# Attention and a two-layer MLP on one core: a join ahead of a difference on VectorE, and one burst of scores behind the first product

## The chip, the cores and the metric

The kernel runs on one core of a Trainium2 chip. The metric is the device time of one execution in microseconds (us). A core has a matrix engine (PE, with its weight loads shown apart as PEld), VectorE (DVE), ScalarE (ACT), GpSimd (POOL) and a queue engine (SP) that here only issues DMAs. Each engine runs its own instructions in program order and waits for the others through semaphores.

## The reference

Eight batches of 12 heads of attention, 448 tokens, head size 64, and then a two-layer MLP with a leaky ReLU over the 3584 rows that come out:

```python
scores = scale * np.matmul(q, k.transpose(0, 1, 3, 2))      # scale = 1/8
attn = softmax(scores)                                       # over the last axis
x = np.matmul(attn, v)      # heads side by side: 3584 x 768
h = x @ w_in                # 768 x 2048
g = np.maximum(0.01 * h, h)
out = g @ w_out             # 2048 x 768, float32
```

## The kernel before, in words

**Units and ranges.** Attention is done by units of two heads: 48 units, each of 4 chunks of scores (112 rows of keys, both heads). The rows of the MLP are done in 7 ranges of tokens, `cuts = [0, 640, 1152, 1664, 2176, 2688, 3072, 3584]`, numbered 0 to 6. Range 0 has 640 tokens, range 5 has 384, the others 512. A range is a short one in this text's code where it has fewer than 512 tokens (`short`, in `block_pair`); the planner's new condition also counts the last range in. While one range is in its second layer, the attention of the ranges after it is computed between its matmuls, so that the exponentials on ACT have matmuls of the MLP beside them.

**First layer.** `hidden(i)` computes h for range i from x transposed (`xT`), by a scheme with seven products in place of eight: blocks of x, and of the weights, are added to and subtracted from each other ahead of the products (`mix_x_part` on DVE, L416, writes `x_mix`). `mix_h` (L441, L442) forms the sums of h that the second layer needs.

**Second layer.** `block_pair(i, c)` computes two blocks of 128 tokens at once, o1 and o2 of 768 columns each, and again with seven products in place of eight. A product is 8 matmuls of 128x384 (L541), with h as the weights that are loaded and `w_out_sb` or its mixed form `w_mix` streaming. There are two PSUM banks for the results, a and b. In the code's order the products write b, a, b, a, b, a, b; products 3, 5, 6 and 7 add onto what their bank holds already. In between, DVE takes the banks' values into o: `keep` copies (L546), `join` adds (L549). `h[:, lo, one]` is overwritten by a difference after product 1 (L553), and `h[:, hi, one]`, which product 2 reads and product 6 reads again, by a difference after product 2 (L558). In the first pair of a short range or of the last range, the `keep` behind product 1 runs on ACT, in all others on DVE. Range 0 has one pair of this kind behind a pair without the scheme (`plain_pair`), the other six ranges have two each: 13 pairs.

A bank may be written again only when what it held has been read: product 3 waits for the `keep` behind product 1, product 4 for the join behind product 2, product 7 for the join behind product 5. DVE runs its queue in order, so an instruction waits for everything queued ahead of it, L416's wait for a transposed x among it.

**Attention between the products.** `second(i)` walks through the pairs of a range. `block_pair` yields after every quarter of a product (two matmuls), and at each yield `place` may put in work for attention: a *burst* of three chunks of scores (six matmuls on PE, L271, into three score tiles of PSUM, and three exponentials on ACT, L280), or the *rows* of one unit (32 matmuls of attention times v, L789, then a reciprocal and a multiply on DVE, L795 and L796, and DMA transposes of x issued on SP, L237). A burst also needs its unit's q and k transposed, by a DMA transpose issued on SP. POOL casts q, k and v and issues the loads.

When a burst is placed is decided when the program is built, by a small model of time in the planner: `model["now"]` grows by 0.325 at each quarter of a product and by 0.78 at a burst, and `free` says for each score tile when it is thought to be free again. `plan = [9, 8, 8, 8, 8, 5, 0]` is the number of bursts that each range is to hold. At the start of each range from 1 on, the model is set back to 0 and every tile's `free` to one value, which is what the second edit changes. A burst is placed when

```python
want > done and state < 2 and turned(last) and not blocked and len(slots) == 3 and all(
    x <= now + 0.05 + 0.2 * j for j, x in enumerate(at)
)
```

with `at` the three tiles' `free` values.

Of the kernel before, what the change touches and what calls it, by code (L numbers as in the profile page):

```python
# [16 lines left out]
def kernel(  # L17
# [13 lines left out]
    P = 128  # L31
# [9 lines left out]
    cuts = [0, 640, 1152, 1664, 2176, 2688, 3072, B * S]  # L41
    NR = len(cuts) - 1
# [24 lines left out]
    slots = [ps_s.tile([P, 2, 512], F32, name=f"sc{i}") for i in range(3)]  # L67
# [253 lines left out]
    def store(o, t0, cols=slice(0, DM), queues=(nc.sync, nc.sync)):  # L321

        queues = list(queues)
        done = 0
        while done < P:
            b, j = divmod(t0 + done, S)
            so, p = divmod(j, SC)
            n = min(SC - p, P - done)
            dst = out[b * S:(b + 1) * S].rearrange("(p so) n -> so p n", so=NSC)
            queues.pop(0).dma_start(out=dst[so, p:p + n, cols], in_=o[done:done + n, cols])  # L330
            done += n
# [87 lines left out]
    def spots(i):  # L419

        if i == 0:
            return 0, [(0, 1), (2, 3)]
        return 0, [(0, 2), (1, 3)] if cuts[i + 1] - cuts[i] == 4 * P else [(0, 1), (KEEP, 2)]

    def token(i, x):

        return KEEP * P if x == KEEP else cuts[i] + x * P
# [96 lines left out]
    def block_pair(i, c):  # L524

        lo, hi = slice(0, MH), slice(MH, MD)
        x1, x2 = spots(i)[1][c]
        one, two = ts(x1, P), ts(x2, P)
        s3 = h_mix[:, :, c]
        t2, t3, t4 = (w_mix[:, x] for x in range(3))  # L530
        t1 = w_out_sb[:, lo, NW:]
        left, right = slice(0, NW), slice(NW, DM)
        o1 = o_pool.tile([P, DM], F32, name="o")
        o2 = o_pool.tile([P, DM], F32, name="o")
        b, a = banks

        def product(ps, x, w, first=False, cols=slice(0, NW)):
            for m in range(MH):
                if m in (2, 4, 6):
                    yield  # L540
                nc.tensor.matmul(  # L541
                    ps[:, cols], x[:, m], w[:, m], start=(first and m == 0), stop=(m == MH - 1), skip_group_check=True,
                )

        def keep(o, at, ps, by=nc.vector.tensor_copy):
            by(o[:, at], ps[:, :NW])  # L546

        def join(o, at, ps):
            nc.vector.tensor_add(o[:, at], o[:, at], ps[:, :NW])  # L549

        yield
        yield from product(b, h[:, lo, one], w_out_sb[:, lo, left], first=True)
        nc.vector.tensor_sub(h[:, lo, one], h[:, lo, two], h[:, lo, one])  # L553
        short = cuts[i + 1] - cuts[i] < 4 * P
        keep(o1, left, b, nc.scalar.copy if c == 0 and (short or i + 1 == NR) else nc.vector.tensor_copy)
        yield
        yield from product(a, h[:, hi, one], w_out_sb[:, hi, left], first=True)
        nc.vector.tensor_sub(h[:, hi, one], h[:, hi, one], h[:, lo, one])  # L558
        join(o1, left, a)
        yield  # L560
        yield from product(b, h[:, lo, one], t2)
        keep(o1, right, b)
        yield
        yield from product(a, h[:, lo, two], t1, first=True)
        keep(o2, right, a)
        yield
        yield from product(b, s3, t3)
        join(o2, right, b)
        yield
        t0 = token(i, x2)  # L570
        last = t0 + P == B * S
        if last:
            nc.vector.tensor_copy(o2[:, NW // 2:NW], b[:, NW // 2:NW])
            store(o1, token(i, x1), left)
            store(o2, t0, right)
        yield from product(a, h[:, hi, one], w_out_sb[:, hi, right])
        join(o1, right, a)
        store(o1, token(i, x1), right if last else slice(0, DM))
        yield
        if last:  # L580
            w1, w2 = slice(0, NW // 2), slice(NW // 2, NW)
            yield from product(b, h[:, hi, two], t4[:, :, w1], cols=w1)
            nc.vector.tensor_copy(o2[:, w1], b[:, w1])
            store(o2, t0, w1, (nc.scalar, nc.sync))
            end = slots[0][:, 0]
            yield from product(end, h[:, hi, two], t4[:, :, w2], first=True, cols=w2)
            nc.vector.tensor_add(o2[:, w2], o2[:, w2], end[:, w2])
            store(o2, t0, w2, (nc.scalar, nc.sync))
            return
        yield from product(b, h[:, hi, two], t4)  # L590
        keep(o2, left, b)
        store(o2, t0)
        banks.reverse()
# [138 lines left out]
    a, b = idle[:, 0], idle[:, 1]  # L732
# [25 lines left out]
    def advance():  # L758
        nonlocal tick
        tick += 1  # L760
        u = to["turn"]
        if u < min(NU, chunk // NSC + NQ, to["cast"]):
            dma_transposes(u)
            to["turn"] += 1
        u = to["cast"]
        if u < min(NU, to["turn"] + 2, to["load"][0], to["load"][1]):
            cast(u, (0, 1))
            to["cast"] += 1
        u = to["v"]
        if u < min(NU, rows_done + NV, to["load"][2]):  # L770
            cast(u, (2,))
            to["v"] += 1
        if tick % 2 == 0:
            x = min(range(3), key=lambda x: to["load"][x])
            u = to["load"][x]
            if u < NU and u - 3 < (to["cast"], to["cast"], to["v"])[x]:
                load_soft(u, 2, (x,))
                to["load"][x] += 2

    def rows():  # L780
        nonlocal rows_done
        u = rows_done
        e, vt = e_sb[u % NE], v_sb[u % NV]
        ps = next_slot()[:, :, :NSC * (D + 1)].rearrange("p j (q d) -> p j q d", q=NSC)
        for j in range(2):
            for qc in range(NSC):
                for c in range(NSC):
                    at = (j * NSC + c) * S + qc * SC
                    nc.tensor.matmul(  # L789
                        ps[:, j, qc, :], e[:, at:at + P], vt[:, j, c, :],  # L790
                        start=(c == 0), stop=(c == NSC - 1),
                    )
        x_t[u] = x_pool.tile([SC, NSC, 2, D], BF16, name="x")
        rec = r_pool.tile([SC, 2, NSC, 1], F32, name="rec2")
        nc.vector.reciprocal(rec, ps[:SC, :, :, D:])  # L795
        nc.vector.tensor_mul(  # L796
            x_t[u].rearrange("p q j d -> p j q d"), ps[:SC, :, :, :D], rec.to_broadcast([SC, 2, NSC, D])
        )
        if u in X_PE:
            owed_x.append((u, model["now"] + 2.0))  # L800
        else:
            x_transposes(u)
        rows_done += 1
# [66 lines left out]
    model = {"now": 0.0, "act": 0.0, "free": {}, "ready": {}}  # L870
# [57 lines left out]
    def second(i):  # L928
# [4 lines left out]
        for c in range(len(spots(i)[1])):  # L933
            whole = c < plain(i)
            for x, _ in enumerate((plain_pair if whole else block_pair)(i, c)):
                fine = 1 if whole else 2
                if x % (2 * fine) == 0:
                    advance()
                if c or x:
                    model["now"] += 0.65 / fine  # L940
                left -= place(i, left, calm=whole or x not in (1, 2), keen=need[min(i + 2, NR)], cap=NU if all(summed) else need[i + 2])
                if whole and x in (1, 3, 5, 7):
                    mix_h(i, x - 1)
                if whole and x in (8, 9, 11, 13, 15):
                    next(outs)
                if i == 0 and c and x % 4 == 2:
                    next(ins, None)
                for y in range(2):
                    if fresh[y] is None and i + 1 < NR and rows_done >= need[i + 2] - 1 + y:
                        fresh[y] = model["now"] + 7.0  # L950
                for y, todo in enumerate(x_sums if x % fine == 0 else ()):
                    if fresh[y] is not None and fresh[y] <= model["now"] and not summed[y]:
                        summed[y] = next(todo, 0) is not None
                        if not summed[y]:
                            break
# [30 lines left out]
    for i in range(1, NR):  # L986
        for step, _ in enumerate(hidden(i)):
            advance()
            if step % 4 == 2 and NSC * (rows_done + 1) <= chunk:
                rows()  # L990
        model.update(now=0.0, act=2.3, free={id(x): 0.9 for x in slots}, ready={})
        second(i)


# [28 lines left out]
```

## Time and profile before

| | |
|---|---|
| time, median of 3 runs | 390.14 us (388.68 to 390.62) |
| time of the profiled execution | 388.9 us |
| span from its first to its last instruction | 387.1 us |
| mean granted clock of TensorE | 0.998 |
| exponentials (L280, ACT) | 192, 163.1 us, mean 918 ns |
| difference L558 (DVE, 128x1024 bf16) | 13, 681 to 1124 ns, median 691 |
| join L549 (DVE, 128x384) | 39, 540 to 555 ns, median 553 |
| keep L546 on DVE / on ACT | 49, median 557 ns / 2, 479 and 492 ns |
| transpose of x or of q and k (SP queue) | one issue takes about 1.2 us |
| loads of q, k, v | 224 KB each, 5.6 to 6.6 us from issue to landing (median) |

The span is counted from the first instruction to the last; the time has what lies around it as well. A line of the timeline gives the start and the duration in us, the engine, the line of the kernel, what is written and read, the number of instructions that are merged in it, and in brackets the idle time of the engine ahead of it with what ended it. TensorE's matmuls overlap, so a merged line's duration is a little longer than the time after which the next one starts; the distance of two starts is the measure. A wait for several semaphores is put down to the one that came last.

### The profile page before, as it was taken

What the parts mean: (1) busy time and instruction counts of PE and PEld (TensorE: products, weight loads), DVE (VectorE), ACT (ScalarE), POOL (GpSimd) and SP (SyncE); (2) the same over time, 40 slices, a digit from 0 to 9 for tenths busy, and PEclk for the clock granted to TensorE, in tenths of its full rate; (3) what the DMA queues carried; (4) which work ended last, traced back from release to release, by engine and by line L of the source; (5) the groups of instructions that cost most, each with busy time, mean ns of one, the idle gap of its engine ahead of it and who ended that gap; (6) DMA issues with size and microseconds to landing.
All of it is one profiled execution on the core that took longest, in us unless ns stands there. A gap on an engine that the chain in (4) does not pass through costs nothing.

```text
span 387.1 us, 10006 instructions
## 1 busy us (share of the span) xinstructions
PE 378.1 (98%) x4093; PEld 262.1 (68%) x4093; DVE 232.7 (60%) x489; ACT 264.9 (68%) x391; POOL 139.9 (36%) x222
## 2 busy tenths in 40 slices
PE   8899999999999999999999999999999999999996
PEld 3565657766588555886558865688656894668854
DVE  3653848566766645766468664665745674464754
ACT  5998885765768776588765887668777686708700
POOL 8797640865537233620436204363042100000000
PEclk9999999999999999999999999999999999999999
DMA  8999999999997969981599815999158500421023
GB/s 131 194 200 203 178 201 182 109 126 199 167 170 91 120 119 137 216 100 25 119 154 180 119 25 93 172 166 141 25 58 192 120 14 1 107 58 50 3 76 88
DMA packets 93246, 46.75 MB, mean 121 GB/s; under 512 B 51856, under 2 KB 89872, under 8 KB 93200
## 3 DMA queue, kind: packets, MB, share of 16 engines
q0 software_dynamic: 38224, 22.58, 46.1%
q1 hardware_dynamic: 54912, 23.50, 31.1%
q8 instruction: 32, 0.52, 0.6%
q14 instruction: 14, 0.11, 0.1%
q10 hardware_dynamic: 64, 0.02, 0.0%
HBM read 45.61 MB, written 11.01 MB: 146 GB/s over the span
## 4 chain that ended last, share of the span: by engine, by line
PE 92%; DVE 2%; DMA 2%; ACT 1%; POOL 1%; issue 1%; POOLq 0%; DVEq 0%; ACTq 0%
PE g L541 31%; PE g L469 14%; PE sc L469 14%; PE sc L789 11%; PE sc L271 10%; PE g L352 4%; PE g L606 3%; PE g L647 2%; DMA w_in_mix<-in_k_dram 2%; PE g L290 2%; PE g L254 1%; ACT e L280 1%; POOL w_in_mix L141 1%; PE sc L352 1%; DVE x L298 1%
## 5 line engine op out<-in xcount | busy, mean ns | idle before, releaser
L280 ACT ACTIVATE e<-sc 112x896 bf16<-112x896 f32 x192 | 163.1, 918 | 50.9 <-PE sc L271 50.7
L541 PEld LDWEIGHTS <-h 128*128 128x128 bf16 x632 | 57.3, 98 | 46.4 <-issue 14.8
L541 PE MATMUL g<-w_out_sb,h 128*128 128x384 bf16 x416 | 80.9, 326 | 0.6 <-DVE o L549 0.6
L458 ACT ACTIVATE h<-c 128x512 bf16<-128x512 f32 (+1 forms) x72 | 43.5, 611 | 25.9 <-DVE c L484 17.3
L469 PEld LDWEIGHTS <-w_in_sb 128*128 128x128 bf16 x576 | 54.3, 98 | 6.0
L789 PEld LDWEIGHTS <-e 112*128 112x128 bf16 x1344 | 48.2, 98 | 4.9 <-ACT e L280 0.7
L172 POOL COPY v<-fv 112x512 bf16<-112x512 bf16 x38 | 24.5, 657 | 74.6 <-PE sc L789 74.6
L271 PE MATMUL sc<-qkT 64*128 64x448 bf16 x384 | 49.9, 355 | 0.7 <-DVE qkT L260 0.5
L789 PE MATMUL sc<-v,e 112*128 112x65 bf16 x1344 | 49.8, 194 | 0.4 <-ACT e L280 0.4
L170 POOL COPY qkb<-fq 112x512 bf16<-112x512 bf16 x38 | 25.1, 660 | 69.0 <-DMA fq<-in_q_dram 38.4
L469 PEld LDWEIGHTS <-w_in_mix 128*128 128x128 bf16 x432 | 41.2, 98 | 4.1
L546 DVE COPY o<-g 128x384 f32<-128x384 f32 x49 | 27.2, 554 | 23.4 <-PE g L541 23.3
L541 PE MATMUL g<-w_mix,h 128*128 128x384 bf16 (+1 forms) x208 | 38.3, 323 | 0.9 <-ACT o L546 0.9
L795 DVE RECIPROCAL rec<-sc 112x8 f32<-112x8 f32 x42 | 8.7, 207 | 42.5 <-PE sc L789 26.9
L271 PEld LDWEIGHTS <-qkT 64*128 64x128 bf16 x384 | 15.4, 94 | 26.6 <-issue 18.7
L170 POOL COPY qkb<-fk 112x512 bf16<-112x512 bf16 x38 | 24.4, 641 | 16.3 <-DMA fk<-in_k_dram 16.3
L549 DVE TENSOR_TENSOR o<-o,g 128x384 f32<-128x384 f32 x39 | 21.5, 551 | 14.2 <-PE g L541 14.1
L796 DVE TENSOR_TENSOR x<-sc,rec 112x512 bf16<-112x512 f32 x42 | 29.0, 691 | 1.7 <-DVE rec L795 0.3
L469 PE MATMUL g<-xT,w_in_sb 128*128 128x256 bf16 (+1 forms) x216 | 28.5, 268 | 0.0
L469 PE MATMUL sc<-xT,w_in_sb 128*128 128x256 bf16 (+1 forms) x216 | 28.5, 268 | 0.0
L541 PE MATMUL g<-w_mix,hmix 128*128 128x384 bf16 x104 | 20.1, 326 | 0.0
L469 PE MATMUL g<-x_mix,w_in_mix 128*128 128x256 bf16 (+1 forms) x144 | 19.0, 268 | 0.0
(102 smaller groups left out, 476.6 us busy)
## 6 DMA issues: line engine op xcount, KB each, us to landing
fq<-in_q_dram POOLq DMA_DIRECT2D x19, 224.0 KB, 5.7
fk<-in_k_dram POOLq DMA_DIRECT2D x19, 224.0 KB, 6.6
fv<-in_v_dram POOLq DMA_DIRECT2D x19, 224.0 KB, 5.6
w_in_sb<-in_moe_w_in_dram POOLq DMA_DIRECT2D x4, 768.0 KB, 11.9
w_out_sb<-in_moe_w_out_dram POOLq DMA_DIRECT2D x4, 768.0 KB, 18.6
out_dram<-o SPq DMA_DIRECT2D x7, 336.0 KB, 4.2
out_dram<-o SPq DMA_DIRECT2D x8, 288.0 KB, 3.3
out_dram<-o SPq DMA_DIRECT2D x7, 240.0 KB, 3.4
```

The costliest lines, as they stand in the source:

```text
L170: by(qk_sb[u][:, x].rearrange("p so h d -> p h so d"), f)
L172: by(v_sb[u % NV][:, :, :, :D], f)
L271: nc.tensor.matmul(ps[:, j, :S], t[j * D:(j + 1) * D, S + c * SC:S + c * SC + P], t[j * D:(j + 1) * D, :S], start=True, stop=True,)
L280: nc.scalar.activation(e[:, :, c, :], sc_t.pop((u, c))[:SC, :, :S], AX.Exp, scale=scale)
L352: nc.tensor.matmul(open_t[m][:, :n], w_in_sb[:, kk, ts(m, P)], xT[:, kk, at:at + n], start=(fresh and kk == kks[0]), stop=(kk == KD - 1),)
L458: nc.scalar.activation(hs[:, m:m + 2, cols], x.rearrange("p (m t) -> p m t", m=2), AX.Prelu, alpha=0.01)
L469: nc.tensor.matmul(ps[:, j * nh:(j + 1) * nh], w[:, kk, ts(j, P)], x[:, kk], start=(first and j == 0 and kk == 0), stop=(kk == KH - 1), sk ...
L541: nc.tensor.matmul(ps[:, cols], x[:, m], w[:, m], start=(first and m == 0), stop=(m == MH - 1), skip_group_check=True,)
L546: by(o[:, at], ps[:, :NW])
L549: nc.vector.tensor_add(o[:, at], o[:, at], ps[:, :NW])
L789: nc.tensor.matmul(ps[:, j, qc, :], e[:, at:at + P], vt[:, j, c, :], start=(c == 0), stop=(c == NSC - 1),)
L796: nc.vector.tensor_mul(x_t[u].rearrange("p q j d -> p j q d"), ps[:SC, :, :, :D], rec.to_broadcast([SC, 2, NSC, D]))
```

## The change

Two edits. In `block_pair`, the join behind product 2 is issued ahead of the difference that overwrites `h[:, hi, one]`; both are on DVE, and nothing is added or left out. In the loop over ranges 1 to 6, the value that the planner gives to the three score tiles at a range's second layer is 0.9 for a range of 512 tokens that isn't the last, as before, and 1.2 for the other two (range 5 with 384 tokens, and range 6, the last).

```diff
         keep(o1, left, b, nc.scalar.copy if c == 0 and (short or i + 1 == NR) else nc.vector.tensor_copy)
         yield
         yield from product(a, h[:, hi, one], w_out_sb[:, hi, left], first=True)
+        join(o1, left, a)
         nc.vector.tensor_sub(h[:, hi, one], h[:, hi, one], h[:, lo, one])
-        join(o1, left, a)
         yield
...
-        model.update(now=0.0, act=2.3, free={id(x): 0.9 for x in slots}, ready={})
+        model.update(now=0.0, act=2.3, free={id(x): 0.9 if cuts[i + 1] - cuts[i] == 4 * P and i + 1 < NR else 1.2 for x in slots}, ready={})
         second(i)
```

The order of the instructions follows from it: on DVE the two instructions change places in each of the 13 pairs. On PE one burst moves, the first one of range 5: two matmuls of product 1 (with their weight loads) that stood behind the burst's six now stand ahead of them. On ACT the copy of o's left half in that pair, which stood behind the burst's three exponentials, stands ahead of them. The orders on POOL and on SP are the same.

## The prediction

> **What bounds the kernel now.** I read the page first, then the chain that ended last, then the waits by engine, and last the timeline around each wait of TensorE that names the two places of the change.
>
> ```profile
> PE 378.1 (98%) x4093; PEld 262.1 (68%) x4093; DVE 232.7 (60%) x489; ACT 264.9 (68%) x391; POOL 139.9 (36%) x222
> PE 92%; DVE 2%; DMA 2%; ACT 1%; POOL 1%; issue 1%; POOLq 0%; DVEq 0%; ACTq 0%
> ...
> PE g L541 <- ACT o L546: 0.9, 1, 0.9
> PE g L541 <- DVE o L549: 0.6, 2, 0.4
> ```
>
> TensorE is the bound: 98% busy, 92% of the chain. DVE and ACT have a third of the span to spare, so moving their work pays only where TensorE waits for it. The last two lines (waits of TensorE: total, times, longest) are all that this view charges to the two orders the change touches: one wait for ACT's copy of o's left half (L546), two for DVE's join (L549). So it is a matter of one or two microseconds, and the timeline must give them exactly.
>
> A product is 8 matmuls. Undisturbed products in the last range start at 368.98, 370.28, 371.58 and 372.88: 1.30 us each, 0.1625 a matmul. A pair's products are numbered 1 to 7 in program order; 1, 3, 5 and 7 write bank b, the others bank a. The join of product 2 must have read a before product 4 may write it. In before it stands behind the difference L558. The four places where TensorE then loses time (start, duration, engine, line):
>
> ```profile
> 96.14 1.46 PE L541 MATMUL g<-w_mix,h 128*128 128x384 bf16 x8
> 96.34 1.12 DVE L558 TENSOR_TENSOR h<-h 128x1024 bf16<-128x1024 bf16 x1 [0.45 <-PE g L541]
> 97.39 0.54 DVE L549 TENSOR_TENSOR o<-o,g 128x384 f32<-128x384 f32 x1
> 97.98 0.48 PE L541 MATMUL g<-w_out_sb,h 128*128 128x384 bf16 x2 [0.38 <-DVE o L549]
> ...
> 320.27 2.53 ACT L280 ACTIVATE e<-sc 112x896 bf16<-112x896 f32 x3 [0.44 <-PE sc L271]
> 320.54 1.80 PE L541 MATMUL g<-w_out_sb,h 128*128 128x384 bf16 x10
> 322.68 0.49 ACT L546 COPY o<-g 128x384 f32<-128x384 f32 x1
> 323.23 1.46 PE L541 MATMUL g<-w_mix,h 128*128 128x384 bf16 x8 [0.89 <-ACT o L546]
> ...
> 339.71 1.46 PE L541 MATMUL g<-w_mix,h 128*128 128x384 bf16 x8
> 340.78 0.55 DVE L549 TENSOR_TENSOR o<-o,g 128x384 f32<-128x384 f32 x1
> 341.38 1.46 PE L541 MATMUL g<-w_out_sb,h 128*128 128x384 bf16 x8 [0.20 <-DVE o L549]
> ...
> 367.51 1.46 PE L541 MATMUL g<-w_mix,h 128*128 128x384 bf16 x8
> 368.38 0.55 DVE L549 TENSOR_TENSOR o<-o,g 128x384 f32<-128x384 f32 x1
> ```
>
> See that product 3 began at 96.14 and was due to hand over at 97.44, but product 4 began at 97.98, right after a join that ended at 97.93.
>
> **Part one, the join ahead of the difference.** It swaps two DVE instructions in each of 13 pairs; nothing is added. The join starts when the difference did and ends one difference earlier (0.69, or 1.12 at 96.34). Where TensorE waited, it stops waiting:
>
> - first range: 97.98 - (96.14 + 1.30) = 0.54. New join 96.34 to 96.89, before 97.44.
> - range 5 (384 tokens), second pair: 341.38 - (339.71 + 1.30) = 0.37. New join 340.18 to 340.73, before 341.01.
> - last range, first pair: 368.98 - (367.51 + 1.30) = 0.17. New join 367.77 to 368.32, before 368.81.
>
> In the other ten pairs the join is early enough, or a burst of scores stands between products 3 and 4, or (range 5, first pair) TensorE waits earlier: worth nothing. The difference itself ends 0.55 later. Its reader is product 6, over 2.5 us behind; the copy of o's right half queued behind it ends when it did, as the two together take as long as before. If that cover were gone, product 5 would wait at most 0.55 a pair.
>
> Now the 0.54 at 98. What is late next there is DVE's own queue. L416 waits for a transpose of x, and the join of product 5 is queued behind it:
>
> ```profile
> 103.08 0.82 DVE L416 TENSOR_TENSOR x_mix<-xT 128x512 bf16<-128x512 bf16 x1 [0.33 <-DMA xT<-x]
> 103.16 1.46 PE L541 MATMUL g<-w_out_sb,h 128*128 128x384 bf16 x8
> 103.82 0.54 DVE L549 TENSOR_TENSOR o<-o,g 128x384 f32<-128x384 f32 x1
> ```
>
> The transposes behind L416 were issued on SP by 97.55, from x that DVE finished at 95.42, ahead of the changed join, so their landing does not move. That join ends at 104.36 as before; product 7, which writes b, was to start at 103.16 + 1.30 = 104.46, and would now be ready at 103.92. It waits until about 104.41. Of 0.54, 0.05 is left. Between the ends 0.05 and 0.54 I take 0.05, since these rows are the place itself.
>
> The Trainium skill, "SBUF — State Buffer", section "SBUF: two separate sides", has a rule against the swap here: a VectorE instruction with two SBUF inputs and a GpSimd one that reads SBUF take a shared port exclusively, and the loser waits for the whole instruction. The difference has two SBUF inputs, and moved to 96.85 it would meet POOL's copy of v at 96.86 (its duration here is 1.07, elsewhere 0.62). The row agrees that they disturb each other (1.12 at 96.34 against a median of 0.691). By the rule the difference would end at 96.86 + 0.62 + 0.69 = 98.17, by the row at 97.97; the copy behind it is not needed before product 5, over 1 us later, so the sum is the same by both.
>
> **Part two, the threshold 0.9 to 1.2.** The planner's clock starts at 0 and goes on by 0.325 at each quarter of a product. At 0.9 the burst fits after three quarters (0.975), at 1.2 only after the whole (1.3). Of the two ranges named, the last has a plan of 0 bursts, so only range 5 changes: two matmuls of product 1 move ahead of the burst (six weight loads and six score matmuls), and on ACT the copy of o's left half moves ahead of the burst's three exponentials. No DMA, no POOL and no SP instruction moves.
>
> Before: copy at 322.68, behind 2.53 us of exponentials; product 3 was due at 320.54 + 10 x 0.1625 = 322.17 and started at 323.23: 1.06 lost. After: product 1 ends its issue at 320.10, its last matmul is through by about 320.30, the copy takes 320.30 to 320.79, and product 3 starts at 322.17. The whole 1.06 is won.
>
> The new price: the exponentials start about 0.42 later and end about 323.22 instead of 322.80, while the second burst comes at 323.56 instead of 324.62. Its three score tiles are released at about 321.6, 322.4 and 323.22 and wanted at 323.56, 323.76 and 323.95: at least 0.73 spare, so nothing. Bounds: 0, and 0.42 if all of that lateness reached TensorE; I take 0 by these rows. Downstream from here no load is outstanding: POOL has no instruction between 318 and 346, and SP's transposes of this stretch start behind the rows they turn. Everything moves with TensorE.
>
> One row is doubtful: the reciprocal at 327.92 starts about 0.36 after the exponential it waits for ends (327.56). Through its multiply, ended at 328.85, it holds the last score tile of the third burst until 328.91, 0.15 late. I take it to move along. If it is tied to time and not to its inputs, TensorE gives 1.06 back there.
>
> **Sum.** 0.05 + 1.06 + 0.37 + 0.17 = 1.65 us off a profiled execution of 388.9 (span 387.1 to 385.45): 387.25, or 0.42%. That execution is 1.24 below the median of the three runs; I carry the difference over to the median: 390.14 - 1.65 = 388.5.
>
> **Rivals.**
>
> - A, nothing is absorbed at 104. Against it: the 0.33 wait of L416. For it: that transpose took 5.5 us from issue to landing, where a lone one at 338.94 took 2.4, so it can land sooner. Then 0.54 counts whole, 2.14 in all, and with the 0.15 at 328.9 gone too 2.29: 387.9 to 388.0.
> - B, the time saved at 322 is given back at 328.9 as above: 1.65 - 1.06 = 0.59, so 389.5. For it: the reciprocal's unexplained 0.36. Against: the same row in the ranges before follows its exponential within 0.02.
> - C, slower: at the same L416 the transposes land later, because POOL's two loads (issued 97.89 and 98.58) get ahead of them when POOL's copies shift beside the moved difference. It decides once the landing is later by more than 1.65, past 104.7. With one load's median of 5.7 us on top of 103.05, TensorE loses 5.7 - 1.65 = 4.1 net: 394.2; at half of that, 391.3. Against: the turn of x is issued 0.34 ahead of the first load.
> - D, the second part does less than it says. That holds for the last range already and is in the sum; for range 5 the order of the instructions decides it.
>
> **How the numbers follow.** Forecast 0.58, A 0.22, B 0.12, C 0.08. Faster by over 0.5% (about what a measurement of this kernel can tell from no change) needs 1.95 us. The forecast stands 0.30 short of that, less than the 0.48 between two of the three runs before: I give it 0.22 faster and 0.36 same. A is just beyond: 0.17 and 0.05. B is 0.12 same, C 0.08 slower. Faster 0.39, same 0.53, slower 0.08. The range reaches down to A less the 1.46 by which the lowest run lies below the median, 386.4, and up to B with the bound of 0.42 and the 0.48 of the highest run, 390.4; C is left out; the forecast's own is 387.0 to 389.0.
>
> **What would show it.** In the profile after: ACT's copy of o ahead of the burst's exponentials near 320.3, no wait of TensorE for L546, and product 3 of that pair following product 2 without a gap; joins ahead of the differences, and no wait of TensorE for a join near 98, 341 or 369; a gap of about half a microsecond before product 7 near 104.4. I am wrong if the second burst near 323.5 waits for an exponential, if the third near 327.5 to 329 holds TensorE by over 0.3, or if L416 near 103 waits for much longer than 0.9.

## The result, and the profile after

The changed kernel took 387.68 us, median of 8 runs, against 389.81 for the kernel before: ratio 0.9941, 95% interval 0.9921 to 0.9961, so 0.59% faster. One of the eight, of 392.64 us, was a slow run that the ratio leaves out; the median of the other seven is 387.56. Measured twice more beside the experiments below, the changed kernel gave ratios of 0.9963 (0.9940 to 0.9987) and 0.9950 (0.9924 to 0.9976). The three agree within their intervals, around half a per cent, which is 1.9 us.

The profiled execution took 388.12, with a span of 386.4, only 0.8 less than before. Where the time went is not read from the two spans but from TensorE's own starts. From the page after, its engines and its chain; then the head of its waits of TensorE:

```profile
PE 378.3 (98%) x4093; PEld 262.8 (68%) x4093; DVE 232.0 (60%) x489; ACT 264.7 (69%) x391; POOL 141.5 (37%) x222
...
PE 94%; DMA 2%; DVE 1%; POOL 1%; ACT 1%; issue 1%; POOLq 0%; DVEq 0%; ACTq 0%
```

```profile
PE g L207 <- DVE gate L202: 1.2, 1, 1.2
PE g L254 <- DVE qkb L170: 1.0, 1, 1.0
PE sc L271 <- DVE qkT L260: 0.5, 1, 0.5
```

The two waits of L541 (for ACT's copy and for the join) are gone from the list. A wait of 1.0 at L254, long before the first changed instruction, was 0.2 before; it ended at 11.95 us, 0.33 later than in the profile before. The windows from 10 to 20 us show what followed it; their columns are the stretch, its length, busy time and count of PE, PEld, DVE, ACT and POOL, then TensorE's granted clock, the DMA share and GB/s. First before, then after:

```profile
10.00:15.00 5.00, 4.03 (x69) 2.79 (x70) 2.85 (x10) 4.84 (x7) 2.56 (x5) 1.00 1.41 187
15.00:20.00 5.00, 4.83 (x83) 3.07 (x81) 3.37 (x11) 4.59 (x7) 5.00 (x9) 1.00 1.29 204
```

```profile
10.00:15.00 5.00, 3.77 (x47) 2.21 (x44) 2.35 (x8) 3.57 (x5) 2.22 (x4) 0.74 1.44 195
15.00:20.00 5.00, 4.83 (x84) 3.48 (x81) 3.27 (x10) 4.38 (x6) 5.00 (x9) 0.92 1.30 204
```

The clock stood at 0.74 and 0.92 where it was 1.00 before; in windows of half a microsecond it was 0.50 from 12.5 to 15.5 us. By 16 us TensorE was 1.1 us late, and it stayed so. Product 1 of the first changed pair shows it, in the timeline before and then in the timeline after:

```profile
91.73 1.46 PE L541 MATMUL g<-w_out_sb,h 128*128 128x384 bf16 x8
```

```profile
92.81 1.46 PE L541 MATMUL g<-w_out_sb,h 128*128 128x384 bf16 x8
```

It starts 1.08 later. From that product to the end of the span the kernel before took 295.4 us and the changed one 293.5, which is 1.9 less. The places where the prediction saw TensorE wait, in the timeline after (start, duration, engine, line; near 98, 104, 322, 341 and 369):

```profile
97.33 1.46 PE L541 MATMUL g<-w_mix,h 128*128 128x384 bf16 x8
97.53 0.56 DVE L549 TENSOR_TENSOR o<-o,g 128x384 f32<-128x384 f32 x1 [0.42 <-PE g L541]
98.63 0.49 PE L541 MATMUL g<-w_out_sb,h 128*128 128x384 bf16 x2
...
103.32 0.42 DVE L416 TENSOR_TENSOR x_mix<-xT 128x512 bf16<-128x512 bf16 x1
103.81 1.46 PE L541 MATMUL g<-w_out_sb,h 128*128 128x384 bf16 x8
104.02 0.56 DVE L549 TENSOR_TENSOR o<-o,g 128x384 f32<-128x384 f32 x1 [0.28 <-PE g L541]
105.11 0.49 PE L541 MATMUL g<-w_mix,h 128*128 128x384 bf16 x2
```

```profile
319.48 1.46 PE L541 MATMUL g<-w_out_sb,h 128*128 128x384 bf16 x8
320.98 0.48 ACT L546 COPY o<-g 128x384 f32<-128x384 f32 x1 [0.46 <-PE g L541]
321.35 2.54 ACT L280 ACTIVATE e<-sc 112x896 bf16<-112x896 f32 x3
321.55 1.48 PE L541 MATMUL g<-w_out_sb,h 128*128 128x384 bf16 x8
322.86 1.46 PE L541 MATMUL g<-w_mix,h 128*128 128x384 bf16 x8
324.25 0.74 PE L271 MATMUL sc<-qkT 64*128 64x448 bf16 x6
```

```profile
339.37 1.46 PE L541 MATMUL g<-w_mix,h 128*128 128x384 bf16 x8
339.84 0.55 DVE L549 TENSOR_TENSOR o<-o,g 128x384 f32<-128x384 f32 x1
340.67 1.46 PE L541 MATMUL g<-w_out_sb,h 128*128 128x384 bf16 x8
...
366.81 1.46 PE L541 MATMUL g<-w_mix,h 128*128 128x384 bf16 x8
367.07 0.56 DVE L549 TENSOR_TENSOR o<-o,g 128x384 f32<-128x384 f32 x1 [0.49 <-PE g L541]
368.11 1.46 PE L541 MATMUL g<-w_out_sb,h 128*128 128x384 bf16 x8
```

See the distances of starts: 97.33 to 98.63, 103.81 to 105.11, 321.55 to 322.86, 339.37 to 340.67 and 366.81 to 368.11 are all 1.30 or 1.31. TensorE loses nothing at any of the five, and the copy of o stands ahead of the exponentials. How late a matmul is against the same matmul of before falls from 1.19 to 0.65 at product 4 near 98, from 0.67 to -0.37 at product 3 near 322, to -0.71 near 341 and to -0.87 near 369: 0.54 + 1.04 + 0.34 + 0.16 = 2.1 us. Elsewhere 0.2 was lost in this execution (0.11 of it at a burst near 96, before any changed instruction).

### The profile page after: what moved, and what is told of

It is laid out like the page before. It is cut to its first block, busy times and chain, and to the rows that moved or that the text cites. A ratio compares the mean times of both kernels' runs of the same rounds, so it can differ in the third digit from the quotient of the medians.

```text
span 386.4 us, 10006 instructions
## 1 busy us (share of the span) xinstructions
PE 378.3 (98%) x4093; PEld 262.8 (68%) x4093; DVE 232.0 (60%) x489; ACT 264.7 (69%) x391; POOL 141.5 (37%) x222
## 4 chain that ended last, share of the span: by engine, by line
PE 94%; DMA 2%; DVE 1%; POOL 1%; ACT 1%; issue 1%; POOLq 0%; DVEq 0%; ACTq 0%
PE g L541 32%; PE g L469 14%; PE sc L469 14%; PE sc L789 11%; PE sc L271 10%; PE g L352 4%; PE g L606 3%; PE g L647 2%; DMA w_in_mix<-in_k_dram 2%; PE g L290 2%; PE g L254 1%; POOL w_in_mix L141 1%; PE sc L352 1%; PE g L317 1%; DVE x L298 0%
## 5 line engine op out<-in xcount | busy, mean ns | idle before, releaser
L541 PEld LDWEIGHTS <-h 128*128 128x128 bf16 x632 | 57.3, 98 | 44.3 <-issue 12.5
L541 PE MATMUL g<-w_out_sb,h 128*128 128x384 bf16 x416 | 80.9, 326 | 0.0
L170 POOL COPY qkb<-fq 112x512 bf16<-112x512 bf16 x38 | 26.0, 684 | 68.2 <-DMA fq<-in_q_dram 37.4
L541 PE MATMUL g<-w_mix,h 128*128 128x384 bf16 (+1 forms) x208 | 38.3, 323 | 0.0
L271 PEld LDWEIGHTS <-qkT 64*128 64x128 bf16 x384 | 15.5, 94 | 26.8 <-issue 18.3
L541 PE MATMUL g<-w_mix,hmix 128*128 128x384 bf16 x104 | 20.1, 326 | 0.0
```

What stands on the lines that cost most here:

```text
L170: by(qk_sb[u][:, x].rearrange("p so h d -> p h so d"), f)
L271: nc.tensor.matmul(ps[:, j, :S], t[j * D:(j + 1) * D, S + c * SC:S + c * SC + P], t[j * D:(j + 1) * D, :S], start=True, stop=True,)
L541: nc.tensor.matmul(ps[:, cols], x[:, m], w[:, m], start=(first and m == 0), stop=(m == MH - 1), skip_group_check=True,)
```

## The experiments

The theory: TensorE's waits at the four places add up, and nothing else is gained. Rivals: the DVE order helps in all 13 pairs; the burst's place, not ACT's queue, is what counts; part of the gain is given back near 104. All runs were profiled, and what each place cost TensorE can be read in each: the distance of two products' starts less 1.30, or for product 3 its lateness behind product 2. Anything up to 0.02 is given as 0.

| kernel | 98: product 4 | 104: product 7 | 322: product 3 | 341: product 4 | 369: product 4 |
|---|---|---|---|---|---|
| before | 0.54 | 0 | 1.05 | 0.37 | 0.17 |
| after | 0 | 0 | 0 | 0 | 0 |
| join alone | 0 | 2.02 | 1.05 | 0 | 0 |
| burst alone | 0.46 | 0 | 0 | 0.37 | 0.17 |
| both, second profile | 0 | 0 | 0 | 0 | 0 |
| both, third profile | 0 | 0 | 0 | 0 | 0 |
| copy on DVE in range 5 | 0.11 | 0 | 0.11 | 0.36 | 0.17 |
| ACT's copy in ranges 1 to 4 too | 0.57 | 0 | 1.05 (five times) | 0.37 | 0.17 |
| short treatment everywhere | 0 | 0 | 0 | 0 | 0 |
| both, product 5's join ahead of L416 | 0 | 0 | 0 | 0 | 0 |
| short treatment and that join | 0 | 0 | 0 | 0 | 0 |

### The burst alone

```diff
-        model.update(now=0.0, act=2.3, free={id(x): 0.9 for x in slots}, ready={})
+        model.update(now=0.0, act=2.3, free={id(x): 0.9 if cuts[i + 1] - cuts[i] == 4 * P and i + 1 < NR else 1.2 for x in slots}, ready={})
```

> Only the second part: the first burst of range 5 behind product 1, joins behind the differences as before. Theory: 1.06 us off, all of it at product 3 near 322; the joins near 98, 341 and 369 hold TensorE by 0.54, 0.37 and 0.17 as before. Rival (the exponentials that now end 0.42 later hold the second or third burst): 0.6 or less off, with a new wait between 323 and 329.

Measured: 387.57 us against 389.07, ratio 0.9967 (0.9948 to 0.9986), so about 1.3 us. In its profile the lateness against the kernel before falls from 0.69 to -0.35 at product 3 near 322, 1.04, and nowhere else behind the first 20 us by more than 0.1; the later exponentials hold no burst. The theory holds.

### The join alone

```diff
+        join(o1, left, a)
         nc.vector.tensor_sub(h[:, hi, one], h[:, hi, one], h[:, lo, one])
-        join(o1, left, a)
```

> Only the first part: the join ahead of the difference in all 13 pairs, the burst where it was. Theory (waits of TensorE add up; the one near 98 us is as long as POOL makes the difference there: 0.54 where it took 1.12 us, 0.11 where it took 0.69): no wait for a join near 98, 341 and 369, so 0.65 to 1.08 us off, with product 3 near 322 still 1.06 late. Rival (the DVE order helps in all pairs): more than 1.6 us off, with differences spread over the ranges.

Measured: 388.52 us against 388.8, ratio 0.9995 (0.9974 to 1.0017). The waits for a join near 98, 341 and 369 are gone and the one near 322 stands at 1.05, as expected, and there is no gain in other pairs. But the profiled execution, the slowest of its twelve (391.97), lost 2.02 at product 7 of range 0. Its timeline there:

```profile
104.64 1.46 PE L541 MATMUL g<-w_out_sb,h 128*128 128x384 bf16 x8
...
106.79 0.65 DVE L416 TENSOR_TENSOR x_mix<-xT 128x512 bf16<-128x512 bf16 x1 [2.56 <-DMA xT<-x]
...
107.36 0.54 DVE L549 TENSOR_TENSOR o<-o,g 128x384 f32<-128x384 f32 x1
...
107.96 0.48 PE L541 MATMUL g<-w_mix,h 128*128 128x384 bf16 x2 [1.85 <-DVE o L549]
```

DVE stood 2.56 at L416 for a transpose of x, with the join of product 5 queued behind it, and TensorE stood 1.85 for that join. This is the prediction's chain at 104, in full, in another execution than the one it was read from. It is also the execution with the lowest early clock of all that were profiled (0.61 from 10 to 15 us, 0.71 from 15 to 20); that the one brings the other is not shown.

The ratio does not resolve the gain, but the clock helps. The mean granted clock of an execution is known for all of them, and 7 of these 12 were below 0.998, against 3 of 19 of the kernel before on this chip. Among those at 0.998 or above, the join alone has a median of 387.82 (5 executions) and the kernel before 388.70 (16): 0.9 us, inside the 0.65 to 1.08 that the places allow. This choice was made after the runs, and 5 are few. Whether an earlier join makes the late transpose more frequent is not shown: it held TensorE in one of the profiles with the join ahead and in none of the others.

### Both again, twice

> The changed kernel once more, for a second profile. Theory: the two parts add up, 2.1 us off where L416 near 103 finds its transpose landed, 1.65 us off where it waits for it and the join of product 5 holds product 7. Rival (the 2.1 of the first profile hung on that execution's late start): near 104 TensorE loses about 0.4 again in an execution whose first range does not start late.

> The changed kernel on the same chip as the kernel with the short ranges' treatment everywhere. Theory: 1.7 to 2.1 us below the kernel before, by how long POOL made the difference near 98 in the kernel before; no wait of TensorE for ACT's copy or for a join, and none of 0.4 at product 7 near 104. Rival (the last part of the gain is given back near 104): a gap there of 0.3 or more.

Measured: 387.8 us against 389.07, ratio 0.9963 (0.9940 to 0.9987), and 386.5 against 388.8, ratio 0.9950 (0.9924 to 0.9976). At a clock of 0.998 or above alone, the medians are 386.58 (4) against 388.78 (19, with one of 1326.82 us left out), 2.2 less, and 386.35 (6) against 388.70 (16), 2.3 less; for the burst alone, 387.42 (10) against the same 388.78, it is 1.4. The third profile, whose early clock is 1.00, answers the question of the late start, since at the burst ahead of product 3 it stands at the same time as the kernel before (0.05 earlier). From there the lateness goes to -0.58 at product 4, to -1.62 near 322, to -1.98 and to -2.15: 0.53 + 1.04 + 0.36 + 0.17 = 2.1, and the span ends 2.1 earlier. Its timeline near 104:

```profile
102.08 0.42 DVE L416 TENSOR_TENSOR x_mix<-xT 128x512 bf16<-128x512 bf16 x1
...
102.58 1.46 PE L541 MATMUL g<-w_out_sb,h 128*128 128x384 bf16 x8
102.78 0.56 DVE L549 TENSOR_TENSOR o<-o,g 128x384 f32<-128x384 f32 x1 [0.28 <-PE g L541]
...
103.88 0.49 PE L541 MATMUL g<-w_mix,h 128*128 128x384 bf16 x2
```

L416 did not wait at all, took 0.42 in place of 0.82, and the join ran as soon as product 5 was through. Nothing is given back. In the second profile L416 did wait (0.28, to 104.13), and product 7 still followed product 6 by 1.30.

### The copy on DVE, the burst left where it was

```diff
-        keep(o1, left, b, nc.scalar.copy if c == 0 and (short or i + 1 == NR) else nc.vector.tensor_copy)
+        keep(o1, left, b, nc.scalar.copy if c == 0 and i + 1 == NR else nc.vector.tensor_copy)
```

> The kernel before, with one copy moved: in range 5, first pair, o's left half is copied by DVE and not by ACT; the burst stays where it was. Theory (TensorE waited for a copy that stood in ACT's queue behind three exponentials): product 3 starts about 0.13 late in place of 1.06, so 0.9 us off, though no burst moves. Rival (the place of the burst among the matmuls is what counts): less than 0.3 us off.

Measured: 388.36 us against 389.07, ratio 0.9978 (0.9953 to 1.0003): the time alone does not decide. The profile does. Its timeline near 322:

```profile
320.84 2.53 ACT L280 ACTIVATE e<-sc 112x896 bf16<-112x896 f32 x3 [0.44 <-PE sc L271]
...
321.11 1.80 PE L541 MATMUL g<-w_out_sb,h 128*128 128x384 bf16 x10
...
322.25 0.55 DVE L546 COPY o<-g 128x384 f32<-128x384 f32 x1
322.85 1.46 PE L541 MATMUL g<-w_mix,h 128*128 128x384 bf16 x8
```

The burst and its exponentials are where they were, yet product 3 starts 0.11 late and not 1.05. It was ACT's queue, not the place of the scores among the matmuls.

### The same wait at four more places

```diff
-        keep(o1, left, b, nc.scalar.copy if c == 0 and (short or i + 1 == NR) else nc.vector.tensor_copy)
+        keep(o1, left, b, nc.scalar.copy if c == 0 else nc.vector.tensor_copy)
```

> The kernel before, with the suspected wait put in at four more places: in ranges 1 to 4 too the first pair's left half of o is copied by ACT, whose queue then holds the burst's three exponentials ahead of it; bursts and joins as before. Theory: product 3 of these four pairs starts 1.06 late in place of 0.11, so 3.8 us slower, 1.0%. Rival (the wait near 322 came from something of range 5 alone, such as its narrower blocks): less than 1 us slower.

Measured: 392.81 us against 388.8, ratio 1.0103 (1.0076 to 1.0130), 4.0 us slower. From its waits of TensorE (total, times, longest):

```profile
PE g L541 <- ACT o L546: 4.4, 5, 0.9
```

Before it was 0.9, once. Five places of the same price (1.05 each by the starts, 0.11 of which the four new ones had before): 4 x 0.94 = 3.8 by the profile, 4.0 by the time. So the wait is not peculiar to range 5.

### The short ranges' treatment everywhere

```diff
-        keep(o1, left, b, nc.scalar.copy if c == 0 and (short or i + 1 == NR) else nc.vector.tensor_copy)
+        keep(o1, left, b, nc.scalar.copy if c == 0 or i + 1 == NR else nc.vector.tensor_copy)
...
-        model.update(now=0.0, act=2.3, free={id(x): 0.9 if cuts[i + 1] - cuts[i] == 4 * P and i + 1 < NR else 1.2 for x in slots}, ready={})
+        model.update(now=0.0, act=2.3, free={id(x): 1.2 for x in slots}, ready={})
```

> The changed kernel with the short ranges' treatment in all of ranges 1 to 6: the first burst behind product 1 (threshold 1.2) and o's left half copied by ACT ahead of it; in the last range the second pair's copy is on ACT too. Theory: the 0.11 that product 3 still waits for DVE's copy near 131, 180, 229, 278 and 376 goes, so 0.55 us below the changed kernel, or more where the wait near 131 is longer. Rival (the exponentials of four more ranges now end 0.4 later and hold the second burst): slower than the changed kernel.

Measured: 385.9 us against 388.8, ratio 0.9934 (0.9909 to 0.9959), 0.6 us below the changed kernel of the same chip (386.5). Its timeline in range 1:

```profile
127.74 0.48 ACT L546 COPY o<-g 128x384 f32<-128x384 f32 x1 [0.35 <-PE g L541]
...
128.12 2.54 ACT L280 ACTIVATE e<-sc 112x896 bf16<-112x896 f32 x3
...
128.31 1.47 PE L541 MATMUL g<-w_out_sb,h 128*128 128x384 bf16 x8
...
129.62 1.46 PE L541 MATMUL g<-w_mix,h 128*128 128x384 bf16 x8
```

Product 3 follows product 2 by 1.31. The 0.11 that the copy on DVE, behind its difference, cost near 131, 180, 229, 278 and 376 is gone at all five, and no later burst waits. Near 131 that wait was not always 0.11: it was 0.15 in the profile after, 0.31 in the burst alone and 0.55 in the second profile of both together, so there the treatment is worth more in some executions.

### The join of product 5 ahead of L416

In the changed kernel, and in the one with the short treatment everywhere, one number of the planner is raised so that in range 0 the join of product 5 stands ahead of the first L416 on DVE; no other engine's order changes.

```diff
-                        fresh[y] = model["now"] + 7.0
+                        fresh[y] = model["now"] + (7.0 if i else 8.0)
```

> The changed kernel with one more step moved on DVE: in range 0 the join of product 5 stands ahead of the first L416, which waits for a transpose of x, and not behind it. Theory (L416's wait, where the transpose lands late, reaches TensorE through that join, 2.0 us in the execution of the join alone): no wait of TensorE at product 7 in any execution, however long L416 waits; the lowest time as for the changed kernel, near 386, and fewer runs above 388. Rival (the late transposes hold TensorE elsewhere, at product 3 of range 1's first layer or at a join behind it): as many high runs as for the changed kernel, and the wait of TensorE moves to about 106 to 109.

> The short ranges' treatment in all of ranges 1 to 6 and the join of product 5 ahead of L416 in range 0, together. Theory: the two add up, 2.6 to 3.1 us below the kernel before, ratio 0.992 to 0.9935, median at most that of the short ranges' treatment alone. Rival: no lower than the changed kernel, 0.994 to 0.996.

Measured: the first 386.79 us against 388.74, ratio 0.9943 (0.9920 to 0.9965), its six runs from 386.54 to 387.26; the second 385.68, ratio 0.9915 (0.9889 to 0.9941), from 385.13 to 386.37. The changed kernel's two later measurements reached 389.92 and 389.3, but those were executions with a clock of 0.991 and 0.990, and all twelve here stood at 0.998 or above: the narrower spread says nothing for the earlier join. In both profiles TensorE waits at none of the five places. In the second the transpose was in time. In the first it landed at 103.31, 0.68 after product 6 had started:

```profile
102.63 1.46 PE L541 MATMUL g<-w_out_sb,h 128*128 128x384 bf16 x8
102.83 0.56 DVE L549 TENSOR_TENSOR o<-o,g 128x384 f32<-128x384 f32 x1 [0.61 <-PE g L541]
103.33 0.43 DVE L416 TENSOR_TENSOR x_mix<-xT 128x512 bf16<-128x512 bf16 x1
...
103.93 0.49 PE L541 MATMUL g<-w_mix,h 128*128 128x384 bf16 x2
```

L416 began as soon as its transpose had landed, with the join already through, and product 7 followed product 6 by 1.30. With L416 ahead of the join, as in the changed kernel, the join would have started near 103.8 and ended near 104.3, and product 7 would have been 0.4 to 0.5 late: an estimate from these rows. So the earlier join was worth that much in this execution, and nothing in the one where the transpose was in time. The second kernel has the lowest ratio of all, 0.85% below the kernel before, but its interval overlaps that of the short treatment alone (0.9909 to 0.9959): the times don't show that the two gains add up.

## Why the prediction was right or wrong

Its time, 388.5 with a range of 386.4 to 390.4, held the result of 387.68. The likeliest case was 0.42% faster; measured were 0.59%, 0.37% and 0.50%. Right in kind, short by one term. Of the 0.8 us between 388.5 and 387.68, 0.33 lies in the kernel before, whose median was 390.14 in the three runs that the prediction started from and 389.81 in the eight of the result; the rest, 0.49, is about that term.

- **The wait for ACT's copy near 322, 1.06.** Right: 1.04 in the burst alone and in the third profile, and its cause is shown by moving the copy to DVE and by repeating the wait four times.
- **The joins near 341 and 369, 0.37 and 0.17.** Right: 0.34 to 0.36 and 0.16 to 0.17.
- **"Of 0.54, 0.05 is left."** This is the step that failed: all three profiles of the changed kernel keep the whole of it, 0.53 to 0.54 where it can be read against the kernel before, so the sum was 2.1 and not 1.65. The chain was right, as the execution with 2.02 shows. Its premise was not, that the landing of the transpose "does not move". In the three profiles L416 began 0.49, 0.14 and 0.50 ahead of product 6, where in before it was 0.08, and it took 0.42 to 0.49 in place of 0.82. One execution's landing and one long L416 were taken for constants. It was not the new order that moved them: in the three other profiles with the join behind the difference (the burst alone, the copy on DVE, ACT's copy in more ranges) L416 also began 0.49 to 0.50 ahead of product 6, waited for no transpose and took 0.42. The transpose took 5.5 us from issue to landing in the profile before, and from 4.7 to 7.1 over all eleven profiles; and the L416 of 0.82 ran beside a copy of POOL's (103.00 to 103.62). Rival A was the case.
- **Nothing for the later exponentials.** Right: in the profile after they end at 323.89 and the third tile is wanted near 324.64, 0.75 spare against the 0.73 foreseen.
- **Nothing for the difference behind the join.** Right: no instruction waits for it in any profile.
- **Rival B, the reciprocal tied to time.** Fell: it moved along, still 0.37 to 0.39 behind its exponential; see the last section.
- **Rival C, slower through a late transpose.** Its place was right and its effect occurs, but not as the usual case: in one of the nine profiles of the experiments, and by the estimate above it would have cost 0.4 to 0.5 in one more. Its reason, loads that get ahead, does not decide it alone: in that execution one load was issued ahead of the transpose (99.27 against 99.63) and the transpose took 7.1 us, but in the second profile of both together it was issued first (97.08 against 97.51) and took 7.0. Why it lands when it does is left open.
- **The Trainium skill, "SBUF — State Buffer", section "SBUF: two separate sides".** Its rule is that a VectorE instruction with two SBUF inputs and GpSimd's copy exclude each other and the one that starts first holds the port. By that rule and the prediction's own starts (96.85 for the difference, 96.86 for the copy) the difference would have held it; the 98.17 was worked out as if POOL did. The traces agree in so far as the two hold each other up: the moved difference took 1.75 us beside three of POOL's copies, of which two kept their 0.62 and the third took 1.08 (the short treatment everywhere), and 0.69 in the third profile of both together, where the copy that began behind it took 1.08. Which of the two holds the port was not to be read from the starts, as in both the difference is shown to begin 0.03 to 0.08 ahead of the copy. As foreseen, nothing on the path waited for it.

On the chances: forecast and rival A lie 0.5 us apart, on either side of the bound of 0.5%, and the three measurements fall on both sides of it as well. The chances for "same" and "faster" were close, as they should be.

## What to carry to other kernels

Where an engine that bounds the kernel waits for a copy, look first at what stands ahead of that copy in its engine's queue: a copy of 0.49 us behind three exponentials cost TensorE 1.05 us here, and the cure was a place in the queue, not a faster copy. Add up the waits of the bounding engine from the distance of its own starts, place by place; the profiled execution of the changed kernel was 1.1 us late, with a lower granted clock, long before the first changed instruction, so look at the clock by windows before two spans are compared. A landing time read from one execution is a sample: price it as a range, and where the order allows it, put what the bounding engine needs ahead of it.

## What the runs showed of the hardware that had not been expected

Part of the spread of the executions goes with TensorE's granted clock in the first 20 us; it is not all of it, since the kernel before ranged from 387.62 to 391.15 on one chip at a mean clock of 0.998 or above. From 10 to 15 us and from 15 to 20 us it was 1.00 and 1.00 in the profiles of before, of both together (third), and of the three kernels with the short treatment or the earlier join; 0.74 and 0.92 in after, 0.66 and 1.00 in the burst alone, 0.72 and 0.93 in the copy on DVE, 0.85 and 0.81 in ACT's copy in more ranges, 0.93 and 0.73 in the second of both, 0.61 and 0.71 in the join alone. In after this makes 0.0044 of the mean clock over the span (0.26 and 0.08 of 5 us each, of 386.4), which is the 0.996 recorded for it. In the third measurement of both together, executions at 0.999 or 1.000 took 385.95 to 386.81, and the two at 0.990 and 0.991 took 389.3 and 388.49. Summed over the two windows the loss is the same, 1.70 to 1.75 us of full clock, in five of the six profiles with a lowered clock, and 3.40 in the join alone; at 0.50, where it stands in windows of half a microsecond, that is 3.4 us and 6.8. In all six TensorE had stood idle for 0.79 to 1.35 us at L254 before, waiting for DVE's copy of a k whose load had just landed; in four of the other five it stood there for at most 0.47. But the kernel with the earlier join alone stood for 0.83 and kept its clock, so a long wait goes ahead of the drop and does not bring it by itself. What does is open. So is the difference in how often it comes (3 of 19 before, 7 of 12 with the join alone on the same chip, but 2 of 8 with both changes there): up to 90 us all these kernels issue the same instructions in the same order.

The wait for the join near 98 is as long as POOL makes the difference ahead of it. In the old order it was 0.11 where the difference took 0.69 (the copy on DVE), 0.46 where it took 1.04, 0.54 where it took 1.12 and 0.57 where it took 1.15: 0.11 plus what it took beyond 0.69, each time. No copy of POOL ran beside the one of 0.69; one or two ran beside each of the others. So this part of the swap is worth 0.1 to 0.6 us by how POOL's copies happen to fall.

In range 5, the reciprocal behind the second burst started 0.37 to 0.39 after the exponential it waits for in the profiles of before, after, the burst alone, the join alone, both again twice, and both with the earlier join; in the copy on DVE, ACT's copy in more ranges and the two kernels with the short treatment everywhere it started 0.01 to 0.02 after it. What sets the second group apart is the number of DVE instructions ahead of it (one more in the first, four fewer in the other three). The timeline of the copy on DVE:

```profile
327.20 0.21 DVE L795 RECIPROCAL rec<-sc 112x8 f32<-112x8 f32 x1 [2.29 <-ACT e L280]
...
328.00 0.74 PE L271 MATMUL sc<-qkT 64*128 64x448 bf16 x6
```

There the third burst takes 0.74, where it takes 0.92 in the profile after: about 0.15 us of TensorE that go with an instruction's position in its engine's stream. What lies behind it no run here shows.
